# Loading two batches of q, k and v through GpSimd's software queue with the cast in the transfer, and operand sums in three pieces

## The chip, the cores and the metric

One Trainium2 chip, one core of it. The metric is the device time of one execution in microseconds (us). The kernel before takes 219.67 us in the median of the four runs beside the changed kernel (217.14 to 220.27). Runs on one core scatter by about 1%, partly because the granted clock of TensorE dips in the first 50 us in some of them; a run over 1.5% above the fastest of its kernel counts as slow and stays out of the ratios.

## The reference, cut to what matters

Four batches of attention (8 heads, 768 positions, head size 64) with a window of 16 and block summaries of 32, then a feed-forward layer with a quick GELU on the 3072 rows:

```python
k_sum = k.reshape(B, H, nb, block, D).max(axis=3)
v_sum = v.reshape(B, H, nb, block, D).mean(axis=3)
# scores in the window of 16 and against the 24 block keys, one softmax over both
x = attn_out.transpose(0, 2, 1, 3).reshape(B * S, H * D)
h = x @ w_in
out = (h / (1.0 + np.exp(-1.702 * h))) @ w_out
```

Inputs and outputs are f32. The kernel computes attention in bf16 and the layer in f16.

## The kernel before

The program runs in eight blocks u of 384 rows, two for each batch. While TensorE does the layer of block u (`ph` with w_in, then `po`, `px`, `pw`, `py` with w_out), the attention of block u + 1 is slipped in. From block 2 on, two thirds of the second product run as a Strassen-like scheme: `g_sums` makes sums of the activations on VectorE (`ssum`, and `gT` in place).

The inputs of batches 2 and 3 come in three steps: the sync queue loads f32, GpSimd casts to bf16, the sync queue transposes k and q by transfer (`kx`, `qT`); the attention result goes back through transposing transfers as well (`xT`, from `dx`).

```python
def xq(g, s):                                   # qT; xk is alike
    sp.dma_start(out=qTs[s][:, 2 * g:2 * g + 2]. ..., in_=qb2[g]. ..., transpose=True)

def pool_after(u):                              # GpSimd waits for the first GELU of block u
    pool.tensor_copy(out=gate2, in_=gT[u % 2][:, 0, 0:1])

def turn_keys(u, b):                            # in block u = 2, 4
    pool_after(u)
    for p in range(NP):
        cast_k(pool, p)
        if p % 2: xk(p // 2, s)
    # ... two q loads, then eight casts of v

def turn_queries(u, s):                         # in block u = 3, 5
    pool_after(u)
    for p in range(NP):
        cast_q(pool, p)
        if p % 2: xq(p // 2, s)

# in the second half of each block, step i:
elif half and b + 2 < B and i == 1:             # blocks 1 and 3
    for p in range(NP): load_k(b + 2, p)        # sync queue, f32
elif half and b + 2 < B and i == 7:
    load_v(b + 2)
elif half == 0 and 0 < b < B - 1 and i == 7:    # blocks 2 and 4
    for p in range(2, NP): load_q(b + 1, p)
```

The softmax here doesn't subtract the row's maximum and nothing guards it: scores larger than these inputs give would overflow.

## Time and profile before

| | before |
|---|---|
| time, median of 4 runs | 219.67 us |
| TensorE busy, 62 to 217 us | 152.32 of 155.00 us |
| k, v and q loads of batch 3, by the sync queue | k from 117.16, v from 129.21, q from 142.58 us |
| GpSimd casts for batches 2 and 3 | 29.0 us |
| first of the two transfers of qT in block 3 | issued at 112.38, waited for until 117.59 us |

TensorE is the bound, and what can be won is in its gaps. A line of an order of time reads: start, duration, engine, line of the program, operation, out<-in with sizes, count, and in square brackets how long the engine sat idle before it and for whom. The lines themselves are in the prediction. "To landing" is the time from the start of the issuing instruction to the arrival of the data. A "run" of 256 B is a contiguous piece of a transfer. The profile of the kernel before fell in a slow run (222.69 us): the clock dipped in the start. From 62 us on the granted clock was 1.00, so the stages argued about here are undisturbed.

### The profile page before, as it was taken

What the parts mean: (1) busy time and instruction counts of PE and PEld (TensorE: products, weight loads), DVE (VectorE), ACT (ScalarE), POOL (GpSimd) and SP (SyncE); (2) the same over time, 40 slices, a digit from 0 to 9 for tenths busy, and PEclk for the clock granted to TensorE, in tenths of its full rate; (3) what the DMA queues carried; (4) which work ended last, traced back from release to release, by engine and by line L of the source; (5) the groups of instructions that cost most, each with busy time, mean ns of one, the idle gap of its engine ahead of it and who ended that gap; (6) DMA issues with size and microseconds to landing.
All of it is one profiled execution on the core that took longest, in us unless ns stands there. A gap on an engine that the chain in (4) does not pass through costs nothing.

```text
span 221.0 us, 5284 instructions
## 1 busy us (share of the span) xinstructions
PE 206.3 (93%) x2078; PEld 130.4 (59%) x2078; DVE 130.3 (59%) x332; ACT 135.2 (61%) x248; POOL 73.3 (33%) x169
## 2 busy tenths in 40 slices
PE   7686987999999999989999989999999999999993
PEld 3355644455665556647666766667667766676672
DVE  5798815453796679593975824466948512822212
ACT  2697666244668667772477747851786678627530
POOL 5685986005695007960410009700500000000000
PEclk9999799799999999999999999999999999999998
DMA  5999999979998999599989999999891510150003
GB/s 152 319 217 186 161 250 226 169 154 222 226 289 250 218 258 234 95 140 193 219 160 221 197 181 231 206 168 247 179 181 30 139 52 0 39 151 27 3 14 130
DMA packets 92857, 37.18 MB, mean 168 GB/s; under 512 B 77872, under 2 KB 89840, under 8 KB 92832
## 3 DMA queue, kind: packets, MB, share of 16 engines
q1 hardware_dynamic: 88416, 31.87, 69.8%
q0 software_dynamic: 4416, 4.98, 13.1%
q8 instruction: 16, 0.26, 0.5%
q14 instruction: 9, 0.07, 0.1%
HBM read 27.26 MB, written 6.29 MB: 152 GB/s over the span
## 4 chain that ended last, share of the span: by engine, by line
PE 66%; DMA 16%; DVE 9%; SPq 4%; issue 1%; POOL 1%; ACT 0%; POOLq 0%
PE ph L28 28%; PE po L28 18%; PE px L28 7%; DMA qfl<-in_q_dram 6%; SPq L28 4%; PE pw L28 4%; DMA xT<-x 3%; DMA vf<-in_v_dram 3%; PE ps_av L28 2%; PE ps_s L28 2%; DMA qT<-qb 2%; DMA kf<-in_k_dram 2%; PE py L28 2%; DVE qT L28 1%; DVE ks L28 1%
## 5 line engine op out<-in xcount | busy, mean ns | idle before, releaser
L28 PE MATMUL ph<-xT,w_in_sb 128*128 128x384 f16 x512 | 86.7, 328 | 1.2 <-DMA xT<-x 0.6
L28 ACT ACTIVATE gT<-ph 128x384 f16<-128x384 f32 x128 | 61.1, 491 | 37.0 <-PE ph L28 36.9
L28 PEld LDWEIGHTS <-w_in_sb 128*128 128x128 f16 x512 | 49.7, 98 | 34.3 <-DMA w_in_sb<-in_moe_w_in_dram 1.6
L28 PE MATMUL po<-w_out_sb,gT 128*128 128x512 f16 x192 | 47.8, 386 | 0.0
L28 PEld LDWEIGHTS <-gT 128*128 128x128 f16 x384 | 36.0, 99 | 19.9 <-issue 1.1
L28 ACT ACTIVATE a_sb<-ps_s 128x768 bf16<-128x768 f32 x32 | 24.3, 805 | 13.7 <-PE ps_s L28 13.7
L28 POOL CAST vw<-vf 128x768 bf16<-128x768 f32 (+4 forms) x35 | 26.2, 791 | 4.8 <-DMA vf<-in_v_dram 3.6
L28 DVE TENSOR_TENSOR ssum<-gT 128x512 f16<-128x512 f16 x12 | 6.4, 534 | 34.3 <-ACT gT L28 34.2
L28 ACT ACT_TABLE_LOAD x16 | 20.5, 1283 | 1.1 <-PEq L1132 0.8
L28 POOL CAST gate<-gT 128x1 bf16<-128x1 f16 x4 | 1.5, 374 | 58.2 <-ACT gT L28 58.2
L28 POOL CAST kb<-kf 128x768 bf16<-128x768 f32 (+1 forms) x15 | 13.5, 925 | 18.4 <-DMA kf<-in_k_dram 18.3
L28 DVE TENSOR_TENSOR a_sb<-a_sb,mk 128x768 bf16<-128x768 bf16 x32 | 17.3, 558 | 3.5 <-ACT a_sb L28 2.7
L28 PEld LDWEIGHTS <-ssum 128*128 128x128 f16 x144 | 14.1, 98 | 5.8 <-issue 0.4
L28 DVE TENSOR_TENSOR x<-ps_av,rc 128x384 f16<-128x384 f32 x28 | 15.6, 558 | 1.0
L28 DVE TENSOR_TENSOR osb<-pw,t 128x256 f32<-128x256 f32 x12 | 5.1, 425 | 16.0 <-PE pw L28 16.0
L28 ACT ACTIVATE t<-px 128x256 f32<-128x256 f32 x12 | 4.6, 381 | 14.1 <-PE px L28 14.1
L28 PE MATMUL px<-ta,ssum 128*128 128x256 f16 x96 | 12.4, 272 | 0.1
L28 DVE COPY kx<-kx 128x80 bf16<-128x80 bf16 (+4 forms) x50 | 12.5, 320 | 0.0
L28 PE MATMUL pw<-tb,gT 128*128 128x256 f16 x96 | 12.5, 273 | 0.0
L28 PE MATMUL ps_av<-vw,a_sb 128*64 128x65 bf16 x384 | 10.7, 199 | 1.2 <-DVE a_sb L28 0.8
L28 PEld LDWEIGHTS <-a_sb 128*64 128x64 bf16 x384 | 8.3, 112 | 6.0 <-DVE a_sb L28 3.0
L28 DVE TENSOR_REDUCE ks<-kx 128x24 bf16<-128x768 bf16 x12 | 11.3, 944 | 0.1
(91 smaller groups left out, 210.6 us busy)
## 6 DMA issues: line engine op xcount, KB each, us to landing
out_dram<-osb SPq DMA_DIRECT2D x22, 256.0 KB, 3.9
kf<-in_k_dram SPq DMA_DIRECT2D x12, 384.0 KB, 6.1
vf<-in_v_dram SPq DMA_DIRECT2D x12, 384.0 KB, 6.3
qf<-in_q_dram SPq DMA_DIRECT2D x8, 384.0 KB, 6.2
w_in_sb<-in_moe_w_in_dram POOLq DMA_DIRECT2D x4, 512.0 KB, 9.1
w_out_sb<-in_moe_w_out_dram POOLq DMA_DIRECT2D x4, 512.0 KB, 17.7
kf<-in_k_dram SPq DMA_DIRECT2D x8, 192.0 KB, 4.5
qfe<-in_q_dram SPq DMA_DIRECT2D x8, 192.0 KB, 3.6
```

Source lines behind the costliest of these rows:

```text
L28: r = f(*a, **kw)
```

## The change

The intent: take 29 us of casts off GpSimd, so that VectorE's sums no longer collide with them; take the f32 loads off the sync queue, so that the transposes go out on time; cut the last sums to an eighth, so that less waits behind the last GELU.

```diff
+    def cast_load(x, b, dst):
+        for h in range(H):
+            pool.dma_start(out=dst[:, h // 2, :, h % 2],
+                           in_=x[b, h].rearrange("(j p) d -> p j d", p=128))
+    # load_kc, load_qc: a new bf16 buffer (one of each), then cast_load
+    def load_vc(b):
+        w5 = vw[b % 2].rearrange("p (j e) h c -> p j e h c", e=2)
+        for j in range(NJ):
+            pool.dma_start(out=w5[:, j, 0, :, 0:D], in_=v[b, :, j * 128:(j + 1) * 128]...)
 ... (single buffers of double size; xk and xq read them)
-    def turn_keys(u, b):
-        pool_after(u)
-        # ... casts of k, xk, loads of q, casts of v
-    def turn_queries(u, s):
-        pool_after(u)
-        # ... casts of q, xq
+    def turn_keys(b):
+        for g in range(2): xk(g, b % 2)
+        v_odd(b)                                # four bf16 copies on GpSimd
+    def turn_queries(b):
+        for g in range(2): xq(g, b % 2)
+    sums = {7: (0, 4), 13: (4, 7), 15: (7, 8)}
-            if u > 1 and nt in (7, NT - 1):
-                g_sums(u, nt // 2 - 3, nt // 2 + 1)
+            if u > 1 and nt in sums:
+                g_sums(u, *sums[nt])
             elif half and b + 2 < B and i == 1:
-                for p in range(NP):
-                    load_k(b + 2, p)
-            # ... load_v at i == 7, load_q in the next block
+                load_kc(b + 2)
+                load_vc(b + 2)
+                load_qc(b + 2)
```

More of the change, by code (lines that the diff above doesn't have):

```diff
@@ L72 @@
     stage = ctx.enter_context(tc.tile_pool(name="stage", bufs=1))
-    castp2 = ctx.enter_context(tc.tile_pool(name="cast2", bufs=2))
+    castp2 = ctx.enter_context(tc.tile_pool(name="cast2", bufs=1))
     attp = ctx.enter_context(tc.tile_pool(name="att", bufs=4))
@@ L127, in load_v, with load_kc, load_qc, v_odd @@
             raw["v", p] = t
+    rows = {}
+    def cast_load(x, b, dst):
+        for h in range(H):
+            pool.dma_start(out=dst[:, h // 2, :, h % 2],
+                           in_=x[b, h].rearrange("(j p) d -> p j d", p=128))
+    def load_kc(b):
+        rows["k"] = castp2.tile([128, NP, NJ, 2, D], BF16, name="kb", tag="kb")
+        cast_load(k, b, rows["k"])
+    def load_qc(b):
+        rows["q"] = castp2.tile([128, NP, NJ, 2, D], BF16, name="qb", tag="qb")
+        cast_load(q, b, rows["q"])
+    def load_vc(b):
+        w5 = vw[b % 2].rearrange("p (j e) h c -> p j e h c", e=2)
+        for j in range(NJ):
+            pool.dma_start(out=w5[:, j, 0, :, 0:D],
+                           in_=v[b, :, j * 128:(j + 1) * 128].rearrange("h p d -> p h d"))
+    def v_odd(b):
+        for p in range(NP):
+            r = rows_of(b % 2, p)
+            pool.tensor_copy(out=r[64:128, :, 1], in_=r[64:128, :, 0])
     ident = consts.tile([128, 128], BF16, name="ident")
@@ L266, in cast_k @@
         else:
-            if p % 2 == 0:
-                kb2[p // 2] = castp2.tile([128, 2, 2, JH, 2, D], BF16, name="kb", tag="kb")
-            t = kb2[p // 2][:, p % 2]
+            if p == 0:
+                kb2[0] = castp2.tile([128, NP, 2, JH, 2, D], BF16, name="kb", tag="kb")
+            t = kb2[0][:, p]
         if half is None:
@@ L280, in cast_q1, with cast_q @@
             cast["q", p, half] = cast.pop(("q", p))
-    def cast_q(eng, p, half=None):
-        if half is None:
-            if p % 2 == 0:
-                qb2[p // 2] = castp2.tile([128, 2, NJ, 2, D], BF16, name="qb", tag="qb")
-            t = qb2[p // 2][:, p % 2]
-        else:
-            g = p // 2
-            if g not in qh or (p, half) in qh[g][1]:
-                qh[g] = castp2.tile([128, 2, NJ, 2, D], BF16, name="qb", tag="qb"), set()
-            qh[g][1].add((p, half))
-            t = qh[g][0][:, p % 2, half * JH:(half + 1) * JH]
+    def cast_q(eng, p, half):
+        if not qh or (p, half) in qh[0][1]:
+            qh[0] = castp2.tile([128, NP, NJ, 2, D], BF16, name="qb", tag="qb"), set()
+        qh[0][1].add((p, half))
+        t = qh[0][0][:, p, half * JH:(half + 1) * JH]
         copy(eng, t.rearrange("p r h d -> p h r d"),
-             raw[("q", p) if half is None else ("q", p, half)])
+             raw["q", p, half])
         cast["q", p] = t
@@ L598, in xk @@
         k4 = kxs[s].rearrange("p i (j e) c -> p (i j) e c", e=2)
-        src = kb2[g].rearrange("p i e r h d -> p (i e r h d)")
+        src = rows["k"][:, 2 * g:2 * g + 2].rearrange("p i j h d -> p (i j h d)")
         for e in range(2):
@@ L605, in xq @@
         sp.dma_start(out=qTs[s][:, 2 * g:2 * g + 2].rearrange("p i (j c) -> p (i j) c", c=128),
-                     in_=qb2[g].rearrange("p i j h d -> p (i j h d)"), transpose=True)
+                     in_=rows["q"][:, 2 * g:2 * g + 2].rearrange("p i j h d -> p (i j h d)"),
+                     transpose=True)
     def rest_k(p, s):
@@ L1011, in pool_after @@
         pool.tensor_copy(out=gate2, in_=gT[u % 2][:, 0, 0:1])
-    def turn_keys(u, b):
-        s = b % 2
-        pool_after(u)
-        for p in range(NP):
-            cast_k(pool, p)
-            if p % 2:
-                xk(p // 2, s)
-        for p in range(2):
-            load_q(b, p)
-        for p in range(NP):
-            cast_v(pool, s, p, 0)
-            cast_v(pool, s, p, 1)
-    def turn_queries(u, s):
-        pool_after(u)
-        for p in range(NP):
-            cast_q(pool, p)
-            if p % 2:
-                xq(p // 2, s)
+    def turn_keys(b):
+        for g in range(2):
+            xk(g, b % 2)
+        v_odd(b)
+    def turn_queries(b):
+        for g in range(2):
+            xq(g, b % 2)
+    sums = {7: (0, 4), 13: (4, 7), 15: (7, 8)}
     for u in range(2 * B):
@@ L1053 @@
         elif half == 0 and b + 1 < B:
-            todo = {0: [lambda: turn_keys(u, b + 1)]}
+            todo = {0: [lambda: turn_keys(b + 1)]}
             if u == 2:
@@ L1058 @@
             s = (b + 1) % 2
-            todo = {0: [lambda: turn_queries(u, s)],
+            todo = {0: [lambda: turn_queries(b + 1)],
                     1: [lambda: rest_k(0, s)], 3: [lambda: rest_k(1, s)],
@@ L1103 @@
             elif half and b + 2 < B and i == 1:
-                for p in range(NP):
-                    load_k(b + 2, p)
-            elif half and b + 2 < B and i == 7:
-                load_v(b + 2)
-            elif half == 0 and 0 < b < B - 1 and i == 7:
-                for p in range(2, NP):
-                    load_q(b + 1, p)
+                load_kc(b + 2)
+                load_vc(b + 2)
+                load_qc(b + 2)
             elif half == 0 and 0 < b < B - 1 and i == 10:
```

## The prediction

> **What bounds the kernel now.** I read the engine table first, then a table of stretches from 62 us on (from the first output block to the end), then TensorE's order of time for its gaps, and last the orders of VectorE, GpSimd and the sync queue around those gaps.
>
> Engine table of the page:
>
> ```profile
> PE 206.3 (93%) x2078; PEld 130.4 (59%) x2078; DVE 130.3 (59%) x332; ACT 135.2 (61%) x248; POOL 73.3 (33%) x169
> ```
>
> Table of stretches; the first number after "length," is TensorE's busy time:
>
> ```profile
> 62.00:82.00 20.00, 19.67 (x253) 11.34 (x252) 14.91 (x31) 14.00 (x20) 7.38 (x30) 1.00 1.02 256
> 82.00:92.00 10.00, 10.00 (x64) 5.89 (x62) 8.63 (x8) 7.93 (x17) 7.80 (x7) 1.00 0.83 177
> 92.00:105.00 13.00, 11.94 (x166) 8.15 (x165) 8.21 (x18) 7.02 (x12) 5.52 (x7) 1.00 1.04 160
> 105.00:116.00 11.00, 11.00 (x72) 6.84 (x71) 9.83 (x28) 6.96 (x15) 3.27 (x5) 1.00 0.95 189
> 116.00:129.00 13.00, 12.55 (x194) 9.08 (x192) 8.97 (x21) 9.60 (x16) 0.00 (x0) 1.00 1.23 195
> 129.00:140.00 11.00, 10.39 (x66) 6.12 (x64) 2.89 (x4) 6.80 (x15) 7.93 (x11) 1.00 1.18 240
> 140.00:152.00 12.00, 11.76 (x166) 8.20 (x165) 7.40 (x18) 6.83 (x12) 2.28 (x3) 1.00 1.12 181
> 152.00:217.00 65.00, 65.00 (x607) 43.48 (x605) 30.87 (x81) 39.55 (x76) 3.30 (x5) 1.00 0.36 85
> ```
>
> From 62 to 217 us TensorE lacks 155.00 - 152.32 = 2.7 us at a granted clock of 1.00: 0.33 before 82, 1.06 in 92 to 105, 0.45 in 116 to 129, 0.61 in 129 to 140, 0.24 in 140 to 152, nothing after. This is the whole stock from which the change can draw: it removes no matmul and touches nothing that runs before about 70 us. 2.7 of 219.47 us is 1.2%. Which wait makes each gap, from TensorE's order of time:
>
> ```profile
> 98.30 0.85 PE L28 MATMUL ps_av<-vw,a_sb 128*64 128x65 bf16 x24 [0.82 <-DVE a_sb L28]
> ...
> 117.63 0.53 PE L28 MATMUL ps_s<-qT,kx 64*128 64x64 bf16 x24 [0.45 <-DMA qT<-qb]
> ...
> 129.88 10.57 PE L28 MATMUL ph<-xT,w_in_sb 128*128 128x384 f16 x64 [0.61 <-DMA xT<-x]
> ```
>
> The first is VectorE being late. It makes the operand sums in the order of its program, then the masks that TensorE wants:
>
> ```profile
> 93.20 0.94 DVE L28 TENSOR_TENSOR ssum<-gT 128x512 f16<-128x512 f16 x1 [2.35 <-ACT gT L28]
> 94.17 0.93 DVE L28 TENSOR_TENSOR ssum<-ssum,gT 128x512 f16<-128x512 f16 x1
> 95.02 1.04 DVE L28 TENSOR_TENSOR gT<-gT 128x512 f16<-128x512 f16 x1
> ...
> 163.70 0.43 DVE L28 TENSOR_TENSOR ssum<-gT 128x512 f16<-128x512 f16 x1 [2.61 <-ACT gT L28]
> ```
>
> The same sum takes 0.94 us at 93 and 0.43 at 163. At 93 GpSimd is casting v (first line below); at 163 it has nothing left to do. The other lines are its transfers with a cast at the start, already in this kernel:
>
> ```profile
> 23.00 0.92 POOL L28 DMA_DIRECT2D qfl<-in_q_dram  x1
> 23.89 3.00 POOL L28 DMA_DIRECT2D w_out_sb<-in_moe_w_out_dram  x4
> ...
> 90.52 7.00 POOL L28 CAST vw<-vf 128x768 bf16<-128x768 f32 x8
> ```
>
> The second and third gap are transposing transfers that start late on the sync queue:
>
> ```profile
> 112.38 4.72 SPq L28 DMA_TRANSPOSE qT<-qb  x2
> 117.16 5.37 SPq L28 DMA_DIRECT2D kf<-in_k_dram  x4
> 123.05 4.65 SPq L28 DMA_TRANSPOSE xT<-x  x2
> ...
> 169.38 3.72 SPq L28 DMA_TRANSPOSE xT<-x  x2
> ```
>
> At 123.05 the first of the two xT issues took 3.32 us, directly behind four k loads, where the usual one takes 1.22 (the median of ten). So the second, whose x was ready at 125.50 (end of the last normalisation on VectorE), went out only at 126.5 and landed at 129.83. At 169, with no loads about, TensorE does not wait.
>
> **What the Trainium skill says.** "SBUF — State Buffer", section "Who interferes with whom": a VectorE instruction with two SBUF inputs contends with a GpSimd instruction that reads SBUF, not with one that only writes. The trace agrees: 0.94 against 0.43 us. "DMA: Bandwidth & Descriptors", section "SWDGE vs HWDGE vs iDMA": a cast in the transfer exists only on GpSimd's queue, and an engine round-robins between its queues. The first fits the kernel; of the second this trace shows no clean case. Same page, section "Issuing engines are not separate DMA queues": all queues end on the same 16 DMA engines, and another issuer saves only issue time. The trace has those engines full already (share 1.23 in 116 to 129). "SBUF — State Buffer", section "SBUF: two separate sides", warns that VectorE in a two-port mode keeps GpSimd from writing descriptors. The issues at 23 to 27 us ran beside VectorE's copies of kx at 0.75 to 0.92 us each, so a large effect does not show.
>
> **The change part by part.**
>
> *Removed from GpSimd:* for batches 2 and 3 each four k casts, eight v casts, four q casts. Batch 2: 5.52 + 7.00 + 3.15 = 15.7 us; batch 3: 3.15 + 7.02 + 3.18 = 13.4 us (its order of time). All lie beside TensorE's work. Also the four waits for gT before them, which cost nothing.
>
> *Added to GpSimd:* 8 loads of k and 8 of q, with 6 x 128 = 768 runs of 256 B each, and 6 of v with 8 x 128 = 1024 runs, per batch. A w_out issue has 512 runs and took 0.75 to 0.78, qfl has 1024 and took 0.92. Estimate from these two: 0.85 us for 768 runs. Per batch 16 x 0.85 + 6 x 0.92 = 19 us, from 69.7 (end of GpSimd's clearing of batch 0's buffers) to about 89 and from about 118 to 137. Then v_odd, four bf16 copies of 64 x 768, an estimated 0.75 us each (a 128x768 cast takes 0.83): 3 us, at about 89 to 92 and 138 to 141. GpSimd's total rises by some 15 us over both batches, off the path.
>
> *Transfers:* the bytes read stay the same, 3 x 1.57 = 4.7 MB per batch. In 69 to 84 us, with the k and v loads running, the DMA view shows 222 GB/s. At that rate a batch needs 21 us, so the end is near 91 and 139, if packets that write 128 B cost no more than those that write 256. Need: k before its transpose, which must not hold up the xT issues at 97.85 and 144.77 (so k at about 90 and 137; expected at about 78 and 126); v before the block sums at 104.4 and 151.2; q before its transpose at 112.4 and 158.8. Every margin is 10 us or more.
>
> *VectorE, sums:* the last batch of sums before the gap falls from 3 instructions of some 0.97 (93.20 to 96.06) to 3 of 0.42 without the collision, and to 3 of some 0.15 (estimate, an eighth of a half with fixed cost) as only one pair of blocks is left after the last GELU. 2.4 us less before the masks; the 0.82 and the 0.2 us beside it at 96.4 vanish. In 140 to 152 the 0.24 vanishes likewise. Cost: 3 more instructions per block, in VectorE's idle time. Sum: 1.2 us.
>
> *qT:* the sync queue was busy without a break from 106.29 to 112.38 with halos, sums and a store. In the next such turn (153 to 158.84), without q loads in front, xq goes out 6.27 us after the first ph, against 6.64 here. So 0.37 us earlier: I count 0.35 of the 0.45.
>
> *xT at 123:* no k loads ahead in its queue, so 1.22 in place of 3.32, and the second issue at 125.5, 1.0 us earlier. But 4.7 MB now come through the other queue, so landing may take 4 us, not 2.8. I count 0.4 of the 0.61.
>
> Sum: 1.2 + 0.35 + 0.4 = 1.95 us. I take off 0.3 for v_odd falling on sums of the first piece and for new gaps of a tenth. 219.47 - 1.65 = 217.8.
>
> **Rivals.**
> 1. *The software queue is slow for short runs* (1,024 descriptors, 128 B written). For: no transfer of this shape is in the trace; the qfl load, 768 B runs, landed after 12.6 us behind other loads. Against: the margins hold even at half the rate. If k landed 10 us late, the kx transpose would hold up xT on the same in-order queue, and each of two turns would stall 3 to 8 us: 224 to 232.
> 2. *The loads collide with transposes.* For: share above 1 in 116 to 140. With 4.7 MB behind one trigger, xT at 125 may land 2 us later than thought, so the gap of 0.61 grows to about 2: 219.5.
> 3. *The gaps close and all 2.7 us come back,* perhaps with a calmer start: 216.8.
> 4. *Nothing shows:* the three runs before span 217.14 to 220.27, which is more than the gain.
>
> **Range and chances.** The gain of 0.2 to 1.2% lies inside the 2% band, and even the whole stock of gaps does not reach 4.4 us, so faster by 2% would need an effect that I don't see: 0.04. Slower by 2% needs rival 1: 0.07. The range of 215.6 to 220.2 joins the mechanism (216.8 to 219.5) with the scatter of the start.
>
> **What would show it.** Right: the sums of blocks 2 and 4 at 0.42 us and the last piece near 0.15; no wait on a_sb near 98; no k, v, q issues on the sync queue after 70 us; a first xT issue near 1.2 us at 122; 44 issues on GpSimd of 0.8 to 0.95 us; TensorE lacking under 1 us from 62 to the end. Wrong: a wait of TensorE on DMA kx, qT or xT of over 1 us, GpSimd issues well over 1 us, or kx transposes that go out after 92 or 140 us.

## More of the kernel before

Every engine's own instructions stay in program order. Between engines there are only the waits for data.

## The result, and the profile after

The changed kernel takes 227.94 us in the median (226.74 to 229.26, four runs), against 219.67. The ratio is 1.040, with a 95% interval of 1.032 to 1.049: slower, above the 215.6 to 220.2 us predicted. A ratio here is the recorded one, over the fast runs of both kernels in the same rounds, so not quite the ratio of the medians. The results are correct.

The two profiles start differently (before is the slow run), so I compare from the first `po` of block 1 to the start of the last `pw`: 66.21 to 216.17 before, 62.27 to 220.66 after. That is 149.96 against 158.39 us, 8.4 us more, which is the whole difference of the medians (8.3).

Stretches of the changed kernel; after the length, TensorE's busy time, and third from the end its granted clock:

```profile
62.27:112.00 49.73, 49.21 (x509) 30.58 (x508) 34.04 (x82) 34.17 (x59) 37.61 (x65) 1.00 1.75 173
112.00:135.00 23.00, 13.44 (x187) 9.09 (x187) 10.89 (x20) 8.52 (x14) 10.35 (x12) 0.85 1.43 120
135.00:221.60 86.60, 86.49 (x831) 57.44 (x829) 39.61 (x114) 53.18 (x102) 0.00 (x0) 1.00 0.35 83
```

Outside of 112 to 135 us TensorE lacks only 0.63 us: the gain that was hoped for is there. Inside it lacks 9.56. TensorE's order of time says for whom:

```profile
119.85 0.82 PE L28 MATMUL ps_s<-qT,kx 64*128 64x64 bf16 x24 [8.03 <-DMA qT<-qb]
120.60 3.03 PE L28 MATMUL po<-w_out_sb,gT 128*128 128x512 f16 x8
...
128.30 0.38 PE L28 MATMUL ps_av<-vw,a_sb 128*64 128x65 bf16 x12 [0.69 <-DVE a_sb L28]
...
133.75 1.03 PE L28 MATMUL pw<-tb,gT 128*128 128x256 f16 x8 [1.03 <-DVE osb L28]
```

The gap of 0.45 us on qT in block 3 has become 8.03. Right after it a group of eight `po` takes 3.03 us where the others take 1.90: in this stretch the granted clock is 0.85. So one late transfer costs 8.03, some 1.1 more at the lower clock that follows, and two smaller waits come behind it. (That the idle time brought the lower clock is not shown: in e1 below a dip followed a wait of 2.10 us, in e7 none followed one of 2.24.)

The sync queue, which issues the transposes:

```profile
107.12 10.79 SPq L28 DMA_TRANSPOSE qT<-qb  x2
126.70 4.24 SPq L28 DMA_TRANSPOSE xT<-x  x2
```

The first qT transpose goes out 6.7 us after the start of the block's `ph` (100.38), as before (112.38 after 105.74). Its issue is not late. Its landing is, by the view of these transfers (12.7 is the first, on which TensorE waits; the second, issued at 112.25, took 10.9):

```profile
DMA to landing us min/median/max: 10.9/11.8/12.7
```

Before, the first took 5.2 us (112.38 to 117.59). What runs beside them is in GpSimd's order of time:

```profile
96.76 6.56 POOL L28 DMA_DIRECT2D kb<-in_k_dram  x8 [8.22 <-DMA kx<-kb]
103.24 2.71 POOL L28 DMA_DIRECT2D vw<-in_v_dram  x3
...
123.70 6.56 POOL L28 DMA_DIRECT2D qb<-in_q_dram  x8 [14.29 <-DMA qT<-qb]
130.19 3.86 POOL L28 COPY vw<-vw 64x768 bf16<-64x768 bf16 x4
```

Batch 3's k and v loads do not start at 118 us, nor in block 3's second half, where the program has them (here from 110.78). They start at 96.76, in block 2, as soon as k's buffer is free. GpSimd has nothing else to do, so its queue runs ahead to the next wait for data: k waits for the kx transposes of batch 2, v for nothing new, q for the qT transposes of block 3. Between 96.76 and 109.4 fourteen loads with 12,288 runs of 256 B are issued. In 104 to 110.5 us the software queue moved 4,641 packets, 714 per us. At that rate they would be through by about 114, but with the transposes beside them they take longer; the last v load, issued at 108.54, is the maximum of the view of the v loads of both batches:

```profile
DMA to landing us min/median/max: 4.9/6.7/14.4
```

So it landed at 122.9, after the first qT transpose (119.8): the loads run right across the transposes. Before, the same k loads stood behind the qT transposes in the sync queue's order, and v behind block 3's xT.

### The profile page after: what moved, and what is told of

Its sections match the earlier page's. It is cut to its first block, busy times and chain, and to the rows that moved or that the text cites. A ratio compares the mean times of both kernels' runs of the same rounds, so it can differ in the third digit from the quotient of the medians.

```text
span 225.0 us, 5298 instructions
## 1 busy us (share of the span) xinstructions
PE 205.1 (91%) x2078; PEld 129.8 (58%) x2078; DVE 125.9 (56%) x350; ACT 135.2 (60%) x248; POOL 86.4 (38%) x185
## 4 chain that ended last, share of the span: by engine, by line
PE 54%; DMA 25%; POOL 9%; DVE 7%; SPq 2%; issue 2%; POOLq 0%; DVEq 0%
PE ph L28 23%; PE po L28 14%; PE px L28 7%; DMA qT<-qb 6%; POOL kb L28 6%; DMA qfl<-in_q_dram 5%; DMA kx<-kb 4%; PE pw L28 3%; DMA qb<-in_q_dram 3%; DMA xT<-x 3%; DMA qfe<-in_q_dram 3%; POOL vw L28 2%; PE ps_s L28 2%; SPq L28 2%; PE ps_av L28 2%
## 5 line engine op out<-in xcount | busy, mean ns | idle before, releaser
L28 DVE TENSOR_TENSOR a_sb<-a_sb,mk 128x768 bf16<-128x768 bf16 x32 | 20.6, 653 | 12.7 <-ACT a_sb L28 11.6
L28 DVE TENSOR_TENSOR ssum<-gT 128x512 f16<-128x512 f16 (+2 forms) x18 | 6.4, 357 | 33.1 <-ACT gT L28 33.1
L28 POOL DMA_DIRECT2D qb<-in_q_dram x16 | 13.2, 866 | 14.4 <-DMA qT<-qb 14.3
L28 PE MATMUL ps_s<-qT,kx 64*128 64x64 bf16 x384 | 9.6, 194 | 9.0 <-DMA qT<-qb 8.0
L28 POOL DMA_DIRECT2D kb<-in_k_dram x16 | 13.1, 862 | 8.3 <-DMA kx<-kb 8.2
L28 PEld LDWEIGHTS <-kx 64*128 64x128 bf16 x384 | 7.3, 96 | 11.3 <-issue 10.4
L28 POOL CAST vw<-vf 128x768 bf16<-128x768 f32 (+4 forms) x19 | 11.9, 667 | 3.6 <-DMA vf<-in_v_dram 1.9
L28 POOL CAST kb<-kf 128x768 bf16<-128x768 f32 (+1 forms) x7 | 4.8, 689 | 17.4 <-DMA kf<-in_k_dram 17.4
```

What stands on the lines that cost most here:

```text
L28: r = f(*a, **kw)
```

## The experiments

Theory A: the loss is a matter of when batch 3's k and v loads run. Theory B: the casting software queue is slow or disturbing in itself. All ratios are to the kernel before in the same rounds. "Stage" is the first `po` of block 1 to the last `pw` as above, from the profiled run; it leaves out the scatter of the start. It rests on one execution each, that of the kernel before on one slow run, and a dip of the clock inside it counts too (e1).

| run | kernel | median us | ratio (95%) | stage us | waits of TensorE over 0.5 us in the stage, for |
|---|---|---|---|---|---|
| – | before | 219.67 | 1 | 149.96 | 0.82 a_sb, 0.61 xT |
| – | changed | 227.94 | 1.040 (1.032 to 1.049) | 158.39 | 8.03 qT, 1.03 osb, 0.69 a_sb |
| e1 | q first | 218.45 | 0.995 (0.988 to 1.002) | 152.03 | 2.10 xT, 1.27 vw |
| e2 | no batch 3 loads | 216.90 | 0.989 (0.982 to 0.997) | slow run | – |
| e3 | finer sums alone | 219.91 | 1.007 (1.001 to 1.013) | 151.73 | 0.82 a_sb, 0.75 qT, 0.70 t, 0.66 xT |
| e4 | v and q late | 217.50 | 0.992 (0.986 to 0.999) | 150.05 | 2.20 qT, 0.60 vw |
| e6 | batch 2 alone | 215.82 | 0.986 (0.975 to 0.997) | 148.21 | none |
| e7 | all paced | 217.05 | 0.995 (0.990 to 1.000) | 149.49 | 2.24 xT |
| e8 | e6, coarse sums | 216.38 | 0.993 (0.988 to 0.998) | 148.36 | none |
| e9 | half of k early | 218.55 | 1.001 (0.992 to 1.009) | slow run | – |
| e10 | e6 again | 216.81 | 0.999 (0.991 to 1.006) | 149.22 | 0.78 vw, 0.52 qT |
| e11 | e9 again | 215.76 | 0.992 (0.985 to 0.998) | 148.61 | 1.39 xT |

### e1: q first

```diff
+                if b + 2 == 3: load_qc(b + 2)
                 load_kc(b + 2)
                 load_vc(b + 2)
-                load_qc(b + 2)
+                if b + 2 == 2: load_qc(b + 2)
```

> Batch 3's loads are issued in the order q, k, v in place of k, v, q. q's buffer is free only when the qT transposes of block 3 have landed, and GpSimd's queue is in order, so k and v now wait for these too. Theory A (the loss is a matter of when batch 3's k and v loads run: nothing on GpSimd's queue holds them back, they start at 97 us and share the DMA engines with the qT transposes): the qT transposes land after about 5 us, not 12.7, TensorE's wait of 8.0 us on qT falls to 0.6 or less, and the time to 218.5 to 220.5; a wait on xT near 125 to 131 may rise to 1.5 us, as the loads now meet those. Theory B (the casting software queue is slow or disturbing in itself, whenever it runs): the loss only moves, to xT or to the kx transposes of batch 3, and the time stays at 224 or above.

218.45 us, ratio 0.995. With q at the head, the in-order queue is held until the qT transposes have landed, and the first load of batch 3 goes out at 113.45 us. These transposes now land after 4.6 and 5.2 us, and no wait on qT is left. Same loads, same cast, same queue: 9.5 us gone by an exchange of order. Theory A foresaw it, theory B did not. The stage in the table, 2 us longer than before, holds three things beside this: a wait of 1.27 us on vw at 70.8 us, before the edited loads run; the wait shown next; and a dip of the granted clock to 0.50 and 0.66 in 127 to 131 us, which makes the 58 matmuls of `ph` take 11.26 us, where they took 9.59 in e7. The loads now meet the next transposes, those of x for block 4, in TensorE's order of time:

```profile
126.19 11.26 PE L28 MATMUL ph<-xT,w_in_sb 128*128 128x384 f16 x58 [2.10 <-DMA xT<-x]
```

That is more than the 1.5 us I allowed for.

### e2: no loads for batch 3

```diff
-            elif half and b + 2 < B and i == 1:
+            elif half and b + 2 < B - 1 and i == 1:
```

> Wrong result on purpose: batch 3 is not loaded, its k, v and q are those of the earlier batches still in the buffers; everything else of the changed kernel stays, batch 2's casting loads and the finer sums too. Theory A: the wait on qT is gone and the time is 216.5 to 218, the floor of what the change could give. Theory B: batch 2's casting loads alone would still cost something, time 220 or above. If batch 2's traffic is harmless this run also says that the whole loss comes from batch 3.

The result is wrong (batch 3 computes with older data). Fast runs: 214.78, 216.22 and 217.58 us, ratio 0.989. So without batch 3's loads the whole loss is gone, and about one per cent on top; batch 2's casting loads with the rest of the change cost nothing that shows.

### e3: the finer sums alone, in the kernel before

```diff
-            if u > 1 and nt in (7, NT - 1):
-                g_sums(u, nt // 2 - 3, nt // 2 + 1)
+            if u > 1 and nt in sums:            # {7: (0, 4), 13: (4, 7), 15: (7, 8)}
+                g_sums(u, *sums[nt])
```

> The kernel before with only the operand sums in finer pieces (half, three eighths, one eighth). GpSimd still casts beside them. The sums after the last GELU fall from 2.9 us to about 0.7 (an eighth, still slowed), so the wait of 0.82 us on a_sb near 98 goes for the most part: 0.5 to 1.1 us less than before, ratio 0.995 to 0.998. If the finer pieces were part of the loss, the ratio would be over 1.

A miss: 219.91 us, ratio 1.007, where I expected 0.995 to 0.998. The gain is not there; that it is slower is not certain, as the rule for slow runs dropped two of the eleven runs of the kernel before and none of these six (medians of all: 219.91 against 219.04). VectorE's order of time shows why nothing was gained, the last piece of block 2's sums:

```profile
90.85 0.84 DVE L28 TENSOR_TENSOR ssum<-gT 128x128 f16<-128x128 f16 x1
91.72 0.74 DVE L28 TENSOR_TENSOR ssum<-ssum,gT 128x128 f16<-128x128 f16 x1
92.38 0.85 DVE L28 TENSOR_TENSOR gT<-gT 128x128 f16<-128x128 f16 x1
```

and the same first instruction in e6, where GpSimd is quiet:

```profile
89.11 0.21 DVE L28 TENSOR_TENSOR ssum<-gT 128x128 f16<-128x128 f16 x1
```

A sum of a quarter of the width takes nearly as long as a sum of 512 did (0.93), and about as long as one of GpSimd's casts (6.79 us for eight), as if each waited for one cast to end: the contention that the prediction cites. Three pieces of 128 take 2.4 us, not 0.65. Under such a lock, cutting an operation into more instructions multiplies the waits. The changed kernel shows the same once: of the three sums of 384 columns in block 2, the one that began beside GpSimd's v_odd copies took 0.74 us, the other two 0.36 and 0.35. So the two parts of the change are not independent: beside the casts, finer sums don't pay.

### e4: v and q late

```diff
                 load_kc(b + 2)
-                load_vc(b + 2); load_qc(b + 2)
+                if b + 2 == 2: load_vc(b + 2); load_qc(b + 2)
 def turn_keys(b):
+    if b == 3: pool_after(4); load_vc(b); load_qc(b)
```

> The changed kernel, but batch 3's v and q loads wait for the first GELU of block 4 (about 130 us); k keeps its early place at 97. Theory A: only k's 6144 short runs (8 us) run before the qT transposes are issued at 107, and nothing runs beside block 3's xT transposes: no wait over 0.6 us on qT or xT, time 217 to 218.5, below both kernels. Theory B: v and q come too late or disturb the kx and xT transposes of block 4: a wait of 2 us or more near 145 to 157, time 220 or above.

217.50 us, ratio 0.992 with the interval below 1: it beats both kernels. But a wait of 2.20 us on qT is left, where I expected under 0.6: k's 6,144 runs, issued from 96.80 to 103.4, are not over when the qT transposes go out at 106.37, and these land after 4.4 and 7.4 us. So k alone makes a quarter of the 8 us, and v, which was in flight for the whole of their time, the rest.

### e5: the transfers by themselves

A kernel with nothing but transfers. Its output is wrong, which doesn't matter for the time. Between phases VectorE reads one element of every target and then writes one of every tile, so that all must have landed. A phase's length is read at VectorE's first wait.

```python
transposes()                 # the two qT transposes, sync queue
software(vb)                 # one batch of v, 6 transfers, GpSimd's queue, cast to bf16
software(vf)                 # the same in f32
hardware(sp); hardware(act)  # the same bytes, sync queue, ScalarE's queue, f32
software(vb); transposes()   # together, and so on for the others
```

> Measures the disputed transfers by themselves, wrong result on purpose. Phases with a full barrier between them: the two qT transposes alone; a batch of v (6144 runs of 256 B) through GpSimd's queue with the cast, through GpSimd's queue in f32, through the sync queue, through ScalarE's queue; then the transposes started together with each of these loads, and last the transposes issued on the sync queue before the loads there. Theory A: all four loads alone take about the same, 8 to 10 us (730 runs per us), the transposes alone about 5 to 6 us, and the transposes beside any load on another queue 9 to 13 us, whether it casts or not; behind loads on their own queue they take as long as load and transpose together. Theory B: the casting load alone takes 1.5 times as long as the f32 one or more, or the transposes beside it land some us later than beside the f32 load on GpSimd's queue or on ScalarE's.

VectorE's order of time, for the end of the transposes alone, of the casting load alone and of the f32 load on the same queue:

```profile
18.85 0.17 DVE L22 CAST mark<-qT 128x4 f32<-128x4 bf16 x1 [5.42 <-DMA qT<-src]
...
28.43 0.17 DVE L22 CAST mark<-vb 128x6 f32<-128x6 bf16 x1 [9.22 <-DMA vb<-in_v_dram]
...
39.28 0.17 DVE L22 COPY mark<-vf 128x6 f32<-128x6 f32 x1 [10.09 <-DMA vf<-in_v_dram]
```

The four ways of loading v alone: cast on GpSimd's queue 9.2 us, f32 there 10.1, sync queue 8.7, ScalarE's queue 8.8. The cast costs nothing that shows; these 6,144 runs take about 9 us or a little more whoever issues them (one reading each). Landing times of the two transposes, alone and beside the casting load:

```profile
DMA to landing us min/median/max: 3.9/4.1/4.2
...
DMA to landing us min/median/max: 5.1/7.5/10.0
```

Beside the f32 load on GpSimd's queue they are 5.8 and 14.5, beside the load on ScalarE's queue 5.4 and 9.6. In front of a load in their own queue they are 3.8 and 4.2, as if alone, and behind one, which is issued first and delays their issue by 4.8 us, 3.8 and 5.6. So each of the three loads on another queue slows the transposes, the casting load no more than a hardware queue's and less than the same load without the cast. Theory B is out. Of the arrangements tried, only the order within one queue protects them, and that is what the sync queue gave before. One number of mine missed: beside the f32 load they took up to 14.5 us, not 9 to 13. There the transfers appear as 480 packets, most of 4 KB, in place of 6,240 small ones, so perhaps a transpose waits for a larger packet at each turn; that is argued, not tested.

### e6, e8, e10: batch 2 alone, with fine and with coarse sums

e6 is the changed kernel with batch 3 on the old path; e8 the same with `sums = {7: (0, 4), 15: (4, 8)}`; e10 repeats e6.

```diff
                 # in the step i == 1, for b + 2 == 3:
+                for p in range(NP): load_k(3, p)        # sync queue, f32, as before
 def turn_keys(b):
+    if b == 3:
+        pool_after(4)
+        # ... casts of k and v on GpSimd, xk, two loads of q, as before; return
 def turn_queries(b):
+    if b == 3:
+        pool_after(5)
+        # ... casts of q on GpSimd, xq, as before; return
```

> The changed kernel with batch 3 loaded the old way: by the sync queue in f32, cast by GpSimd after the gates. Batch 2 keeps the casting loads, the finer sums stay. Theory A: no wait on qT over 0.6 us, time 217.5 to 219.5, at or a little below before. Theory B: half of the loss or more stays, 222 or above.

> e6 with the operand sums in two halves as before. In e6 the sums after the last GELU of block 2 took 0.65 us with GpSimd quiet; in e3, beside GpSimd's casts, 2.4. If the finer pieces gain once the casts are gone, this is 0.2 to 0.8 us slower than e6; if GpSimd's silence alone made the gain, it is the same as e6 within 0.2 us.

> e6 once more (batch 3 the old way), for a comparison with e9 on the same chip in the same rounds and with e8 by more runs: 215.5 to 216.5, ratio to before 0.986 to 0.993.

e6: 215.82 us, ratio 0.986, below the 217.5 to 219.5 expected; e10, the same kernel in other rounds: 216.81, ratio 0.999, both above what I expected of it (215.5 to 216.5, 0.986 to 0.993). The kernel before scattered in those rounds so far (216.29 to 220.97) that five of its eleven runs counted as slow and fell out of the ratio. All fast runs of e6 and e10 taken together average 216.64 us, those of the kernel before beside them 218.49, ratio 0.991. e8: 216.38, ratio 0.993. The stage agrees: 148.21 and 149.22 with fine sums, 148.36 with coarse ones. So batch 2's part of the change gains a little under 1%, as the prediction's mechanism said, and the finer sums add nothing that these runs can show (under 0.2 us in the stage against e6, expected 0.2 to 0.8). The gain fits GpSimd's silence while VectorE sums (no wait on a_sb near 98 in any of the three) and qT transposes that are no longer waited for in block 3; the runs don't separate the two. The stage accounts for 0.7 to 1.75 us of the 1.85 between the averages; whether the start of the kernel changed too is not tested.

### e7, e9, e11: batch 3 through the software queue, paced

e7 adds to e4 a GpSimd copy that reads a column of qT before k's loads, so that k waits for the landing of the qT transposes. e9 and e11 (the same kernel) load k of heads 0 to 3 at once and hold the rest with v and q until block 4:

```diff
 # e7, before load_kc(3)
+                pool.tensor_copy(out=gate2, in_=qTs[0][:, NP - 1, 0:1])
 # e9, e11
+                cast_load(k, 3, rows["k"], range(4))       # in place of load_kc(3)
 def turn_keys(b):
     if b == 3:
         pool_after(4)
+        cast_load(k, b, rows["k"], range(4, 8))
         load_vc(b); load_qc(b)
```

> The changed kernel with batch 3's casting loads paced by data: k waits for the landing of block 3's qT transposes (about 112 us), v and q for the first GELU of block 4 (about 125 us). Theory A: qT lands undisturbed (the 2.2 us wait of e4 was k's own 6144 runs), xT of block 3 meets only the end of k's 8 us; no wait of TensorE over 0.6 us after 75 us, time 215 to 217, at or below e6. Theory B (casting loads cost more than f32 loads by the sync queue even when paced): 1.5 us or more above e6, 217.3 or above.

> The changed kernel with batch 3's casting loads cut to the gaps between the transposes: k of heads 0 to 3 at once (97 us, 3072 runs, 4 us), k of heads 4 to 7, then v and q after the first GELU of block 4 (125 us). Theory A: in e4 the whole of k (8 us) ran into qT and cost 2.2 us, in e7 into xT of block 3 and cost 2.2; half of k is over before qT starts at 106 us and nothing runs beside xT: no wait over 0.6 us, time 215 to 216.5, level with e6 of this call within 0.5 us. Theory B: at least 1.5 us above e6.

> e9's kernel once more, because e9's profile fell in the slow state (granted clock 0.753), where TensorE is slower and the transfers are not, so that it can't show whether a wait on a transfer is left. Theory A: a profile in the fast state has no wait of TensorE on qT or xT over 0.6 us after 75 us; by e9's fast runs (216.06 to 218.94) the time is 216 to 219. If a wait on the kx, xT or vw transfers of block 4 or 5 of over 1 us is there, cutting k in half only moved the collision.

e7: 217.05 us, ratio 0.995. qT is undisturbed, but k's loads, issued from 112.99 to 119.5, now meet the xT transposes issued at 116.36, and TensorE waits 2.24 us for xT. I had counted on 0.6 at most. e9 gave no reading: its profile is of a slow run (265 us at a granted clock of 0.753), and its fast runs, 216.06 to 218.94, missed the 216.5 that I had set as the upper end. e11 repeats it: 215.76 us, ratio 0.992, nothing waited for on qT, but a wait of 1.39 us on the xT transposes that are issued in block 4:

```profile
135.50 4.97 SPq L28 DMA_TRANSPOSE xT<-x  x2
...
144.49 1.15 PE L28 MATMUL ph<-xT,w_in_sb 128*128 128x384 f16 x6 [0.18 <-DMA xT<-x]
147.03 9.59 PE L28 MATMUL ph<-xT,w_in_sb 128*128 128x384 f16 x58 [1.39 <-DMA xT<-x]
```

Both went out as soon as VectorE had their x ready (at 135.50 and 139.25), so nothing in front of them in the sync queue held them. They landed some 8.9 and 7.7 us later, where 2.8 is their time without loads about, while v's and q's loads, issued from 127.77 to 140.7, were in flight. The kx transposes in front took 11.96 us from the first to the last, but 6.0 of that is the second pair's wait for its own half of k, which this edit holds back; no wait of TensorE over 0.3 us came of it. That is the case "only moved the collision" of its expectation. Of the five ways tried to place 18,432 runs (the changed kernel, e1, e4, e7, e11), each makes some transpose pay: qT, xT of block 3, or xT of block 4. The time doesn't settle what this is worth: e9 and e11 are one kernel, with ratios 1.001 and 0.992; their eight fast runs average 217.01 us against 218.09 of the kernel before beside them, 0.995.

## Why the prediction was wrong

- **What bounds the kernel, and the stock of 2.7 us:** right. Outside of 112 to 135 us TensorE in the changed kernel lacks 0.63 us, where the kernel before lacked 1.63 outside of 116 to 140, and e6 reached a stage 1.75 us shorter than before.
- **VectorE's sums:** right in mechanism. The sums of 512 took 0.42 us in block 2, the last piece 0.22 each where I estimated 0.15, and the wait of 0.82 us on a_sb near 98 is gone. That the finer pieces contribute to this is not borne out (e8), and by themselves they gain nothing (e3).
- **GpSimd's issues:** right, 0.86 us in the median for k against 0.85 estimated.
- **The step that failed:** "from 69.7 ... to about 89 and from about 118 to 137". For batch 3 I read the place in the program as a time. 118 us was when the sync queue had come to its k loads, because they stood in order behind the qT transposes. GpSimd's queue carries no such neighbours, and the loads started at 96.76 us. Where the loads are held until the qT transposes have landed (e1, from 113.45), the time is 218.45 us, near the predicted 217.8. The change also took away two gates per batch, but they would not have given the old pace: the gate of block 3 opens with the end of its first GELU, at about 102.4 us in the changed kernel, and k's loads would still have gone out before qT at 107.12. No run kept the gates.
- **"Every margin is 10 us or more":** true for when the loads are needed, and beside the point. The question not asked was what the loads do to the transposes that run meanwhile: 5.2 us became 12.7, and instead of the 0.35 us to be won on qT, the wait on it grew from 0.45 to 8.03, with about 1.1 at a lower clock and 1.7 in two waits behind it.
- **The xT part:** the first issue took 1.21 us, as forecast, and there was no wait. After a stall of 8 us this says little about the gain of 0.4 counted there.
- **The two waits behind it** are only argued: during the 1.03 us on osb, VectorE's two masks at 129.85 took 3.52 us beside GpSimd's v copies (usually 1.02 to 1.26), and the other, on a_sb, falls beside q's issues.
- **The rivals:** the second named the collision, but with xT, and of 2 us. That is what e1 and e7 show. The first, a slow software queue, is refuted by e5. The rate, taken from loads on the sync queue, was off by some 20%: 714 runs of 256 B per us are 183 GB/s, not 222.

What stays open: whether any placement of batch 3's casting loads is free of collisions, and whether any beats leaving batch 3 as it was. By the fast runs e4 is 0.8% below the kernel before, e9 and e11 together 0.5%, and e6 and e10, with half of the change, 0.9%; these runs can't order them.

## What to carry to other kernels

When a transfer moves from a busy in-order queue to an idle one, it loses its pace: it starts when its buffer is free, not where the program has it. Look for the last wait for data in front of it, ask which latency-critical transfers are in flight at that time, and hold it with a read of their result if need be; then look which transfers it meets next (e7 met xT). And a piece that waits for a lock is not made shorter by cutting it: first remove the lock.

## What the Trainium skill lacked or had wrong

- "DMA: Bandwidth & Descriptors", section "Rules for kernel authors", says that a transpose next to ordinary DMAs needs nothing. That concerns correctness, and all results here were correct; in time, two transposes that land after 3.9 and 4.2 us alone took 5.1 and 10.0 beside one batch of v (e5), and 12.7 and 10.9 in the changed kernel.
- The same page, section "Queues, rings and completion order", has the round robin between queues by packets, but no number for what a short transfer loses by it: beside 4 KB packets (the f32 load on GpSimd's queue) the slower of the two transposes took 14.5 us, beside loads in some 6,200 short packets 9.6 to 10.0.
- The same page, section "Bandwidth", gives GpSimd's queue in measured rates by the size of a transfer, but none for a load in 256 B runs: 6,144 of them, 1.57 MB, took 9.2 us through GpSimd's queue with the cast and 10.1 without, 8.7 and 8.8 through the sync queue and ScalarE's. How this changes with the length of a run is not tested.
- "SBUF — State Buffer", section "SBUF: two separate sides", says that the loser blocks for the whole instruction, which e3 fits; it doesn't say that finer pieces then cost more: three sums of 128 columns took 2.4 us beside casts of 0.85, and 0.65 without.
